# A recurrent cell fused with a gated layer: the first two slots of four chunks in another order, and the last store in halves

## The chip, the cores and the metric

The kernel runs on one core of one Trainium2 chip. A core has a matrix engine (PE, with its weight loads shown as PEld), a vector engine (DVE), an activation engine (ACT), a general engine (POOL), and a queue engine (SP) that issues most transfers; ACT and POOL issue some too. Each engine works through its own list of instructions in order and waits on semaphores for the others. Matrix products land in PSUM, everything else lives in SBUF. The metric is the device time of one execution in microseconds; the median of the runs is compared. The granted clock of PE is 1.00 in every stretch of the profile that is quoted here.

## The reference

An mLSTM cell runs over 4 batches, 8 heads and 768 time steps with head size 40; its output, with heads and batch folded, is the input of a feed-forward layer whose activation is `h * cos(h)`.

```python
for t in range(S):
    m_new = max(f[t] + m, i[t])
    f_stab, i_stab = exp(f[t] + m - m_new), exp(i[t] - m_new)
    C = f_stab * C + i_stab * outer(v[t], k[t])
    n = f_stab * n + i_stab * k[t]
    y[t] = sigmoid(o[t]) * (C @ q[t]) / max(abs(n . q[t]), 1)
x = y as (3072, 320)
h = x @ w_in            # 320 -> 2048
out = (h * cos(h)) @ w_out   # 2048 -> 320
```

## The kernel before

**Chunks and cells.** Time is cut into six chunks of 128 steps (`NC` = 6, `C` = 128). A *cell* n = (chunk, batch) is computed in the parallel form of the recurrence: scores of keys against queries (`scores`, L560), times decays (`weigh`, L566), times values plus the carried state (`values`, L586 to L595), a division by the denominator (`normalize_turned`), and an update of the state: `seam` (L701) makes the increment in PSUM, `fade` (L684, POOL) decays the state `st`, `state` (L726, DVE) adds the increment. The last chunk's cells need no new state. `weigh_k` (L481) and `odd_values` (L487) prepare keys and the odd part of the values on POOL; `turn_blocks` (L538) transposes queries and keys on DVE; `scale_q` (L542, POOL) multiplies queries by the carried decay; `decay` (L476) takes exponentials on ACT.

**The layer, one chunk behind.** While the cells of chunk c + 1 are made, the layer runs on chunk c. Its 2048 hidden columns are done in eight *slots* `f2` = 0 to 7 of 256 columns, two to each batch `b`, the first with `i == 0`, the second with `i == 1`. From the third chunk on (`fast` = 2) `both_parts_fast` does this. In each slot, in this order on PE: the up products of a seven-product scheme (`UpFast`, L817 and L833), with two products of the way down as filler between them; in the even slots the cell's `values` and `seam`; then the slot's share of products of the way down (`down_slot`, L1013). In the second slot these are the sixteen *late* products of the chunk before, and the next cell's scores follow them.

**The other engines in a slot.** ACT copies parts of the up products out of PSUM (L825, L826); POOL adds them up (L834 to L836); DVE joins them into the rest (`join`, L842 and L844). Then the nearest whole number of turns is taken (`near`, L757 on ACT), subtracted (`rest`, L760 on DVE), the sine follows (`sin`, L765 on ACT) and the product with h (`gate`: L769 on DVE for one half, L852 on POOL for the other). `sums` (L902 to L905, four adds on POOL or DVE) forms the combinations of two batches that the way down needs. `x_sums` (L801 to L804, POOL) does the like for the next chunk's input, in the eighth slot. `seam_out` (L708) sends a part of the new input from SBUF to SBUF by two transfers on ACT's queue in the odd slots; they stand between the roundings and the sines.

**The order is written by hand.** `tc.manual_schedule()` keeps each engine's instructions in the order of the calls. Where a call stands in `both_parts_fast` sets its place in the list of its engine; waits are added where one instruction needs another. PSUM buffers are taken in turn from small pools: cells use two buffers of `ps_a`, so the two score tiles of the next cell take the buffers of the last cell's values and of its state increment, and the up products use two of `ps_u`.

**The end.** For the last chunk `last_products` lists the products by `k` (the slot) in an order of its own, and `combine_last` adds them up on DVE (`add_turns`, L875) and stores four blocks of 128 tokens and 320 columns: three from SP (L881), the last one from ACT (L1008). The accumulators are `X0`, `X1`, `Y0`, `Y1`, the tile `late` of two column halves, and `own`.

Of the kernel before, what the change touches and what calls it, by code (L numbers as in the profile page):

```python
# [29 lines left out]
def kernel(  # L30
# [20 lines left out]
    nc = tc.nc  # L51

    B, H, S, D = q.shape
    C = 128
# [3 lines left out]
    D1 = D + 1  # L58
# [878 lines left out]
    def last_products():  # L937

        c = NC - 1
        acc[c] = [ps_o.tile([128, 3, HALF], FP, name="acc", tag="o") for _ in range(4)]  # L940
        late[c] = ps_a.tile([128, 2, HALF], FP, name="late", tag="a")
        own[c] = ps_a.tile([128, HALF], FP, name="own", tag="a")
        X0, X1, Y0, Y1 = acc[c]
        L, Z = late[c], own[c].unsqueeze(1)
        T2, T3, T4 = T

        def first(k):
            G0, G1 = (gs[c, 2 * k + e].rearrange("q (p e t) -> q p e t", p=2, e=2) for e in range(2))
            S, B = blocks[:, S_of(c, k):S_of(c, k) + 4], [[wv[:, k, e, h] for h in range(2)] for e in range(2)]
            return [(X0, 0, G0[:, 0, 0], B[0][0]), (X0, 1, G1[:, 0, 0], B[1][0]), (X0, 2, S[:, 0], T2[:, k]),  # L950
                    (Y0, 0, G0[:, 0, 1], T3[:, k]), (Y0, 1, G1[:, 0, 1], T4[:, k]), (Y0, 2, S[:, 2], B[0][1]),
                    (Y1, 1, S[:, 3], B[1][1])]

        def second(k):
            G0, G1 = (gs[c, 2 * k + e].rearrange("q (p e t) -> q p e t", p=2, e=2) for e in range(2))
            S, B = blocks[:, S_of(c, k):S_of(c, k) + 4], [[wv[:, k, e, h] for h in range(2)] for e in range(2)]
            D1, D4 = (blocks[:, D_of(c, k) + i] for i in range(2))
            return [[(X1, 0, G0[:, 1, 0], B[0][0]), (X1, 1, G1[:, 1, 0], B[1][0]), (X1, 2, S[:, 1], T2[:, k])],
                    [(Y1, 0, G0[:, 1, 1], T3[:, k])], [(L, 0, D1, B[0][1]), (L, 1, D4, B[1][1])],
                    [(Z, 0, G1[:, 1, 1], T4[:, k])]]  # L960

        def ordered():
            for k in range(LAST - 1):
                yield from first(k)
                for part in second(k):
                    yield from part
            yield from first(LAST - 1)
            yield from first(LAST)
            for part in zip(second(LAST - 1), second(LAST)):
                for some in part:  # L970
                    yield from some

        left = {id(t): NF // 2 * n for t, n in ((X0, 3), (X1, 3), (Y0, 3), (Y1, 2), (L, 2), (Z, 1))}
        begun = set()
        for t, i, lhs, rhs in ordered():
            left[id(t)] -= 1
            yield t[:, i], lhs, rhs, id(t) not in begun, left[id(t)] == 0
            begun.add(id(t))
# [3 lines left out]
    def combine_last():  # L982
        c = NC - 1
        X0, X1, Y0, Y1 = acc[c]
        lo, hi = slice(0, HALF), slice(HALF, DM)

        def spread_first(X):
            o = [out_tile() for _ in range(2)]
            nc.scalar.activation(out=o[1][:, lo], in_=X[:, 0], func=AF.Copy, scale=TWO_PI)
            add_turns(out=o[0].rearrange("q (h n) -> q h n", h=2), in0=X[:, 1:3], in1=o[1][:, lo].unsqueeze(1).to_broadcast([128, 2, HALF]))  # L990
            return o

        o = spread_first(X0)
        add_turns(out=o[1][:, hi], in0=Y0[:, 0], in1=o[0][:, hi])
        add_turns(out=o[1].rearrange("q (h n) -> q h n", h=2), in0=Y0[:, 1:3], in1=o[1][:, hi].unsqueeze(1).to_broadcast([128, 2, HALF]))
        out_to(c, 1, o[1])
        add_turns(out=o[0][:, hi], in0=Y0[:, 2], in1=o[0][:, hi])
        p = spread_first(X1)
        add_turns(out=o[0][:, hi], in0=Y1[:, 1], in1=o[0][:, hi])
        out_to(c, 0, o[0])  # L1000
        o, L = p, late[c]
        add_turns(out=o[1][:, lo], in0=Y1[:, 0], in1=o[0][:, hi])
        add_turns(out=o[1][:, hi], in0=L[:, 0], in1=o[1][:, lo])
        add_turns(out=o[0][:, hi], in0=L[:, 0], in1=o[0][:, hi])
        add_turns(out=o[0][:, hi], in0=L[:, 1], in1=o[0][:, hi])
        out_to(c, 2, o[0])
        add_turns(out=o[1][:, lo], in0=own[c], in1=o[1][:, lo])
        nc.scalar.dma_start(out=out[3 * S + c * C:3 * S + (c + 1) * C], in_=o[1])  # L1008

    def run(made, n):  # L1010
        for _ in range(n):
# [489 lines left out]
    def both_parts_fast(c, b):  # L1501

        n = (c + 1) * B + b
        cell, follows = n < N, n + 1 < N
        first = (c, b) == (fast, 0)
        ahead = {0: 3, B - 1: 2}.get(b, H - 2)
        pool = nc.gpsimd if cell else nc.vector
        for i in range(2):
            f2 = 2 * b + i
            up = UpFast(c, f2, lambda: fill_in(c, f2))  # L1510
            if f2 == 0:
                if cell:
                    place_gates(c + 1)
                if cell and not first:
                    odd_values(n)
                    weigh_k(n)
                sin_next()
            if f2 == 2 * B - 2 and c + 2 < NC:
                sigmoid_in_place(c + 2)
                sin_next()  # L1520
            if cell and i == 0:
                if first:
                    scores(n)
                    scale_q(n)
                else:
                    values(n)
                    seam(n)
                    if f2 > 0 and follows:
                        turn_blocks(n + 1)
                if follows:  # L1530
                    decay_exponents(n + 1)
            if cell and i == 1:
                if follows:
                    decay(n + 1, range(ahead, H))
                    sin_next()
                    if f2 > 1:
                        scores(n + 1)
                if n % 2 == 1 and n + 3 < N:
                    load_two(n + 3)
                if b == B - 1:  # L1540
                    x_sums(c + 1)
                elif follows:
                    weigh_k(n + 1)
                    odd_values(n + 1)
                    scale_q(n + 1)
            up.join()
            for e in range(2):
                up.near(e)
            for e in range(2):
                up.rest(e)  # L1550
            if first and i == 0:
                weigh(n)
            if f2 == 2 and cell:
                combine_late(c - 1)
            if cell and i == 0 and not first:
                fade(n)
            if cell and i == 1:
                seam_out(n)
            for e in range(2):
                up.sin(e)  # L1560
                up.gate(e)
            if f2 == 0 and follows:
                turn_blocks(n + 1)
            if f2 == 0:
                sums(c, 0, pool)
            if f2 == 2:
                sums(c, 1, pool)
            down_slot(c, f2)
            if f2 == 1 and follows:
                scores(n + 1)  # L1570
            if f2 == 0:
                for p in range(2):
                    combine_first(c - 1, p)
                for p in range(2):
                    combine_x(c - 1, p)
            if cell and i == 0:
                if follows:
                    decay(n + 1, range(ahead))
                if first:
                    values(n)  # L1580
                    seam(n)
                    fade(n)
                normalize_turned(n)
                if n + 2 < N:
                    load_blocks(n + 2)
                if n + 3 < N:
                    load_E(n + 3)
                if b == B - 2 and c + 2 < NC:
                    load_o(c + 2)
            if i == 0:  # L1590
                if cell:
                    state(n)
                if f2 > 0:
                    sums(c, f2)
            if i == 1:
                if follows:
                    if b == B - 1:
                        scale_q(n + 1)
                    weigh(n + 1)
                if b == 0:  # L1600
                    combine_y(c - 1)
                    if not cell:
                        combine_late(c - 1)
                else:
                    sums(c, f2)
# [42 lines left out]
```

## Time and profile before

| | us |
|---|---|
| median of 3 runs (lowest, highest) | 505.79 (505.65, 506.99) |
| profiled execution | 507.92 |
| its span | 506.1 |
| PE busy | 495.6 (98%) |
| DVE busy | 423.4 (84%) |
| ACT busy | 332.9 (66%) |
| POOL busy | 299.4 (59%) |

The profiled execution is 1.8 us longer than its span, and 2.1 us longer than the median of the three runs. Times inside the profile are counted from the span's start. Two columns of the timeline matter: the start of a group of equal instructions and the time from its start to its end; where an engine stood idle before a group, brackets say for how long and what it waited for. Line numbers name the line of the kernel that issued an instruction; a helper such as `run` (L1013) issues products for many callers, so the tile names tell which ones they are (`acc`, `late`, `own` for the way down; `pup` for the way up).

### The profile page before, as it was taken

Reading aid. Unit: us, or ns where it says so; the run is one execution under the profiler, and the core shown is the slowest. Engines: PE = TensorE matmul, PEld = TensorE weight load, DVE = VectorE, ACT = ScalarE, POOL = GpSimd, SP = SyncE. Lnnn points to the kernel's source line nnn. Section 1 sums busy time; section 2 is a strip of 40 time slices with the busy share of each in tenths; the row PEclk is TensorE's granted clock in tenths of the full one; section 3 lists DMA queues with packets and bytes.
Section 4 is the critical chain, followed back from the end, with each engine's and each line's share of the span. In section 5 each row is a group of like instructions: output and inputs, shape, how many; then the busy total and the mean of one; then the engine's idle time right before and its main releaser. Section 6 shows DMA issues by size and latency. Waiting matters only on the chain.

```text
span 506.1 us, 11146 instructions
## 1 busy us (share of the span) xinstructions
PE 495.6 (98%) x4038; PEld 374.6 (74%) x4038; DVE 423.4 (84%) x842; ACT 332.9 (66%) x646; POOL 299.4 (59%) x394
## 2 busy tenths in 40 slices
PE   9999999999999999999999999999999999999996
PEld 6856645465667668887887788788688878787876
DVE  7889987999887888899889989889979966777655
ACT  6799988888554576754877756777747643444541
POOL 8354656575645666877657967666857456434340
PEclk9999999999999999999999999999999999999999
DMA  9988899998366436129546119628113000010001
GB/s 140 178 215 235 208 219 249 227 230 167 96 172 118 114 109 136 49 77 196 142 116 115 43 42 209 168 70 161 43 33 85 1 6 5 2 53 0 2 0 54
DMA packets 100519, 56.74 MB, mean 112 GB/s; under 512 B 63440, under 2 KB 93216, under 8 KB 100464
## 3 DMA queue, kind: packets, MB, share of 16 engines
q1 hardware_dynamic: 97408, 54.43, 46.7%
q10 hardware_dynamic: 2752, 1.23, 0.9%
q8 instruction: 32, 0.52, 0.5%
q0 software_dynamic: 304, 0.36, 0.3%
q14 instruction: 23, 0.19, 0.1%
HBM read 50.66 MB, written 4.10 MB: 108 GB/s over the span
## 4 chain that ended last, share of the span: by engine, by line
PE 65%; DMA 10%; DVE 9%; SPq 6%; ACT 5%; issue 3%; POOL 1%; ACTq 0%; DVEq 0%
PE acc L1013 19%; PE pup L817 14%; PE pup L749 7%; PE pup L833 5%; PE late L1013 4%; DMA blocks<-in_moe_w_in_dram 4%; PE ps L560 3%; PE po L863 3%; DMA kr<-in_k_dram 2%; PE pup L743 2%; DMA vs<-in_v_dram 2%; DVE n L760 2%; ACT n L757 2%; PE vt L595 2%; PE vt L586 1%
## 5 line engine op out<-in xcount | busy, mean ns | idle before, releaser
L757 ACT ACTIVATE n<-pup 128x512 int32<-128x512 f32 x64 | 36.9, 594 | 85.9 <-DVE pup L842 61.2
L852 POOL TENSOR_TENSOR g<-g,n 128x512 f32<-128x512 f32 x31 | 39.6, 1276 | 54.0 <-ACT n L765 52.0
L765 ACT ACTIVATE n<-n 128x512 f32<-128x512 f32 x96 | 57.9, 627 | 17.2 <-DVE n L760 11.8
L749 PE MATMUL pup<-xT,w_in_sb 128*128 128x512 f32 x128 | 58.8, 602 | 2.2 <-DVE g L769 2.0
L760 DVE SCALAR_TENSOR_TENSOR n<-pup,n 128x512 f32<-128x512 f32 x64 | 43.1, 689 | 19.8 <-ACT n L757 17.5
L1013 PE MATMUL acc<-w_out_sb,g 128*128 128x160 f32 x320 | 58.5, 302 | 0.0
L1013 PE MATMUL acc<-T,g 128*128 128x160 f32 x304 | 56.4, 301 | 0.0
L834 POOL TENSOR_TENSOR blocks<-blocks 128x256 f32<-128x256 f32 x32 | 25.7, 803 | 50.7 <-ACT blocks L826 50.7
L817 PE MATMUL pup<-xT,w_in_sb 128*128 128x256 f32 x192 | 53.5, 385 | 0.2
L476 ACT ACTIVATE E<-E,tab 128x128 f32<-128x128 f32 x160 | 50.1, 389 | 4.3 <-POOL E L462 4.1
L1013 PEld LDWEIGHTS acc<-w_out_sb,g 128*128 128x128 f32 x320 | 49.0, 190 | 4.5 <-issue 2.7
L749 PEld LDWEIGHTS pup<-xT,w_in_sb 128*128 128x128 f32 x128 | 23.0, 189 | 32.9 <-issue 32.2
L1013 PEld LDWEIGHTS acc<-T,g 128*128 128x128 f32 x304 | 46.5, 190 | 1.1 <-issue 0.4
L769 DVE TENSOR_TENSOR g<-pup,n 128x512 f32<-128x512 f32 x64 | 42.7, 687 | 5.2 <-ACT n L765 4.4
L817 PEld LDWEIGHTS pup<-xT,w_in_sb 128*128 128x128 f32 x192 | 33.6, 189 | 9.7 <-ACT blocks L826 4.5
L825 ACT COPY blocks<-pup 128x512 f32<-128x512 f32 x32 | 18.7, 583 | 32.3 <-PE pup L817 32.2
L817 PE MATMUL pup<-x_room,room 128*128 128x256 f32 x128 | 38.5, 382 | 0.0
L1013 PE MATMUL acc<-T,blocks 128*128 128x160 f32 x160 | 36.2, 308 | 0.2 <-POOL blocks L904 0.2
L863 PE MATMUL po<-w_out_sb,g 128*128 128x320 f32 x128 | 36.2, 436 | 0.1
L833 PE MATMUL pup<-xL,w_in_l 64*128 64x512 f32 x128 | 36.1, 641 | 0.0
L542 POOL TENSOR_TENSOR qG<-t,G 128x512 f32<-128x512 f32 x20 | 25.5, 1277 | 16.7 <-DVE t L538 16.7
L1013 PE MATMUL acc<-w_out_sb,blocks 128*128 128x160 f32 x160 | 33.8, 301 | 0.0
(227 smaller groups left out, 1208.3 us busy)
## 6 DMA issues: line engine op xcount, KB each, us to landing
E<-M_d SPq DMA_DIRECT2D x20, 512.0 KB, 6.2
qr<-in_q_dram SPq DMA_DIRECT2D x72, 80.0 KB, 2.5
kr<-in_k_dram SPq DMA_DIRECT2D x72, 80.0 KB, 2.1
bits<-in_moe_w_out_dram SPq DMA_DIRECT2D x8, 640.0 KB, 6.8
G<-G_d SPq DMA_DIRECT2D x18, 256.0 KB, 6.4
blocks<-in_moe_w_in_dram SPq DMA_DIRECT2D x32, 128.0 KB, 4.6
out_dram<-o_sb SPq DMA_DIRECT2D x23, 160.0 KB, 1.8
o<-in_o_gate_dram SPq DMA_DIRECT2D x40, 80.0 KB, 3.9
```

Source lines behind the costliest of these rows:

```text
L476: nc.scalar.activation(out=Es[n][:, h], in_=Es[n][:, h], func=AF.Exp, scale=-1.0, bias=tab[:, c, 0, g:g + 1])
L749: nc.tensor.matmul(pu.rearrange("p (b t) -> p b t", b=B), w_in_sb[:, i, ts(2 * f2 + e, 128)], xT[c][:, i:NK * B:NK], start=(i == 0 and not ...
L757: nc.scalar.activation(out=self.n[e], in_=self.pu[e], func=AF.Copy, bias=0.25)
L760: nc.vector.scalar_tensor_tensor(out=self.n[e].bitcast(FP), in0=self.pu[e], scalar=0.25, in1=self.n[e], op0=OP.add, op1=OP.subtract)
L765: nc.scalar.activation(out=r, in_=r, func=AF.Sin, scale=TWO_PI_DOWN)
L769: nc.vector.tensor_tensor(out=g, in0=self.pu[e], in1=self.n[e].bitcast(FP), op=OP.mult)
L817: nc.tensor.matmul(bank[:, part].rearrange("p (b t) -> p b t", b=B // 2), w[:, f2], x, start=start, stop=stop, skip_group_check=True)
L833: nc.tensor.matmul(pu, w_in_l[r, f2], xL[c][r].rearrange("p b t -> p (b t)"), start=False, stop=True, skip_group_check=True)
L834: nc.gpsimd.tensor_tensor(out=s[:, 1], in0=s[:, 1], in1=s[:, 0], op=OP.add)
L852: tt(out=self.g, in0=self.g, in1=self.n[e].bitcast(FP), op=OP.mult)
L863: nc.tensor.matmul(po[c][b], gs[c, f][:, ts(b, C)], w_out_sb[:, f], start=(f == 0), stop=(f == NF - 1))
L1013: nc.tensor.matmul(a, lhs, rhs, start=start, stop=stop)
```

## The change

In `both_parts_fast`, that is in chunks three to six:

- `weigh` of the very first cell stands before the rounding of its slot, not behind it.
- `odd_values` of a chunk's first cell is called at the end of the eighth slot before it, where `scale_q` stood; `scale_q` is called right after `x_sums` in that slot. Before, `odd_values` stood behind the up products of the first slot.
- `sums(c, 0)` on POOL, and `fade` of the very first cell, are called in the second slot behind `scale_q`, not at the end of the first slot. In chunk six, which has no cells, `sums(c, 0)` stays where it was, on DVE.
- `state` of each chunk's first cell is called in the second slot, behind the gate, not at the end of the first one. In the later batches it stays.

In `last_products` the four late products of the last two slots come by column half. In `combine_last` the last block's right half is stored as soon as it is added up, and the left half at the end; before, one store took both.

```diff
-                    [(Y1, 0, G0[:, 1, 1], T3[:, k])], [(L, 0, D1, B[0][1]), (L, 1, D4, B[1][1])],
+                    [(Y1, 0, G0[:, 1, 1], T3[:, k])], [(L, 0, D1, B[0][1])], [(L, 1, D4, B[1][1])],
...
         add_turns(out=o[1][:, hi], in0=L[:, 0], in1=o[1][:, lo])
+        nc.scalar.dma_start(out=out[3 * S + c * C:3 * S + (c + 1) * C, hi], in_=o[1][:, hi])
...
-        nc.scalar.dma_start(out=out[3 * S + c * C:3 * S + (c + 1) * C], in_=o[1])
+        nc.scalar.dma_start(out=out[3 * S + c * C:3 * S + (c + 1) * C, lo], in_=o[1][:, lo])
...
                 if cell and not first:
-                    odd_values(n)
                     weigh_k(n)
...
                 if b == B - 1:
                     x_sums(c + 1)
+                    if follows:
+                        scale_q(n + 1)
                 elif follows:
                     weigh_k(n + 1)
                     odd_values(n + 1)
                     scale_q(n + 1)
+                if b == 0:
+                    if first:
+                        fade(n)
+                    sums(c, 0, pool)
             up.join()
+            if first and i == 0:
+                weigh(n)
             for e in range(2):
                 up.near(e)
             for e in range(2):
                 up.rest(e)
-            if first and i == 0:
-                weigh(n)
...
             if f2 == 0 and follows:
                 turn_blocks(n + 1)
-            if f2 == 0:
+            if f2 == 1 and cell:
+                state(n)
+            if f2 == 0 and not cell:
                 sums(c, 0, pool)
...
                 if first:
                     values(n)
                     seam(n)
-                    fade(n)
...
             if i == 0:
-                if cell:
-                    state(n)
                 if f2 > 0:
+                    if cell:
+                        state(n)
                     sums(c, f2)
             if i == 1:
                 if follows:
                     if b == B - 1:
-                        scale_q(n + 1)
+                        odd_values(n + 1)
                     weigh(n + 1)
```

## The prediction

> **What bounds the kernel now.** I read the engine table first, then what the matrix engine (PE) waited for from the third chunk on, then the timeline around each of those waits, and last the tail. Names: a *chunk* is 128 time steps, chunk three to six are c = 2 to 5 and start on PE at 194.3, 273.3, 351.9 and about 429; each has eight *slots* of about 10 us, and the change works in the first two.
>
> ```profile
> PE 495.6 (98%) x4038; PEld 374.6 (74%) x4038; DVE 423.4 (84%) x842; ACT 332.9 (66%) x646; POOL 299.4 (59%) x394
> ...
> PE vt L589 <- POOL vr L487: 0.7, 2, 0.4
> PE pup L817 <- ACT blocks L825: 0.5, 1, 0.5
> PE vt L586 <- DVE E L566: 0.4, 1, 0.4
> PE late L1013 <- DVE o_sb L875: 0.3, 1, 0.3
> ```
>
> PE is busy 98% of the span, so DVE, ACT and POOL cost only where PE stands. The other lines (matrix engine's waits from 194 us on: us in all, times, longest) hold about 2 us; four of the six waits lie in the slots that the change reorders. The timeline shows more loss than "idle", because matmul ends are modelled; I count from start to start. In chunk five:
>
> ```profile
> 357.36 0.40 PE L586 MATMUL vt<-E,vs 128*32 128x128 f32 x8
> 357.57 0.40 PE L595 MATMUL vt<-qG,st 128*32 128x128 f32 x8
> 358.34 0.43 PE L589 MATMUL vt<-E,vr 128*32 128x128 f32 x8 [0.37 <-POOL vr L487]
> ...
> 363.14 0.43 PE L1013 MATMUL acc<-T,g 128*128 128x160 f32 x2
> 363.41 0.43 PE L1013 MATMUL acc<-w_out_sb,blocks 128*128 128x160 f32 x2
> 364.38 0.48 PE L817 MATMUL pup<-x_room,w_in_sb 128*128 128x256 f32 x1 [0.54 <-ACT blocks L825]
> ```
>
> Groups of L586/L595 follow each other at 0.22 us; L589 comes 0.77 after its forerunner, so 0.55 is lost. Products of two passes follow at 0.27; L817 comes after 0.97, so 0.70 is lost. The same two places lose 0.55 (279.77) and 0.27 (285.31 to 285.85) in chunk four; chunk three loses 0.52 at 202.74. Together 2.6 us: the most that the slots can give.
>
> Next, the second slot of chunk four on DVE and ACT, and the scores on PE that end it:
>
> ```profile
> 288.30 0.86 DVE L726 TENSOR_TENSOR st<-st,pu 40x128 f32<-40x128 f32 x4
> 289.23 0.43 DVE L842 TENSOR_TENSOR pup<-pup,blocks 128x256 f32<-128x256 f32 x1
> 292.67 0.69 DVE L769 TENSOR_TENSOR g<-pup,n 128x512 f32<-128x512 f32 x1 [0.21 <-ACT n L765]
> ...
> 289.69 0.60 ACT L757 ACTIVATE n<-pup 128x512 int32<-128x512 f32 x1 [0.43 <-DVE pup L842]
> ...
> 293.00 1.16 PE L560 MATMUL ps<-t,t 40*128 40x128 f32 x16
> ```
>
> Today the state adds (L726) end at 289.16, four us ahead of the scores that reuse their PSUM buffer. The gate L769 ends at 293.36, after the scores begin. The change puts the adds behind that gate.
>
> **The change part by part.**
>
> *Chunk three, weights before the rounding.* The two L566 (1.27) go ahead of the two L760. L844 ends at 200.27 and the scores at 200.02, so the first L566 ends about 200.95, before PE arrives (about 202.2): the 0.52 goes. The price: ACT's two sines end at about 203.6 for 202.75, which eats the 0.82 that L825 of the second slot idles today; it starts at 206.4 for 206.26, ends 207.0, and the product behind it can start at 207.05 for 207.42. PE gains about 0.35 there, no more.
>
> *Odd values and scale_q, chunks four and five.* L487 moves from the first slot to the end of the eighth one before, so the 0.55 goes. L542 (1.28) moves ahead of the gate L852 there. DVE's L760 at 350.97 waits today for POOL's L804 (ends 351.24) and runs 0.55 after it; L542 then starts at about 351.8 and ends at 353.1, and the gate starts 0.34 late (352.73 today), ending at 354.35. PE's second filler product, at 354.15, waits for that: 0.2. What follows on DVE:
>
> ```profile
> 354.05 1.48 DVE L902 TENSOR_TENSOR blocks<-g 128x256 f32<-128x256 f32 x1
> 355.56 0.83 DVE L903 TENSOR_TENSOR g<-g 128x256 f32<-128x256 f32 x1
> ...
> 194.73 0.42 DVE L902 TENSOR_TENSOR blocks<-g 128x256 f32<-128x256 f32 x1
> ```
>
> Each of these takes 0.42 with POOL idle (chunk three), 0.83 beside a POOL add, 1.48 beside L542. Without L542, the four (354.05 to 358.13 today) end at about 357.35, 0.75 earlier although L902 starts 0.3 later; but the second join L844 also needs POOL's L836, which I get to 358.0 for 357.86, so L844 starts at about 358.05 for 358.39. Rounding, sines, exponentials and the copy L825 follow in order, so L825 comes 0.35 earlier (bounds 0.1 and 0.75). PE, freed of the 0.55 less 0.2, arrives before it: it gains 0.35 in both chunks, and still waits.
>
> *Sums, fade and state.* The four sums of POOL (L902 to L905, 2.9 us) go from the end of slot one to slot two, behind L542; in chunk three the four fades (1.4) too. POOL then starts L834 as soon as L826 has landed (1.8 us sooner in chunk four: 285.8 for 287.65), and DVE reaches the join without 0.86 of adds. So ACT alone sets the rounding: from L825 to L757 it needs 4.03 (285.24 to the end of the table load and the 0.20 behind it, 289.26). From L757 on: 0.62 to the second, 1.20 to the sine (ACT issues two L708 transfers, 1.12), 0.66 to the gate, 0.69, then four adds 0.87: 4.04. The last add ends 8.07 after L825; unheld, the second pair of scores comes 7.75 after it (7.15 from product to scores, 0.6 before). New wait: PE stands about 0.35 to 0.4, with the rest of the scores and all of slot three queued behind, on DVE L566 and on POOL the next adds.
> Chunk three: L825 at 206.4, adds done 214.5 to 214.85 (there today's sine comes 1.41 behind the second L757, the late end), against today's 214.56 for that pair: 0.15 lost. Bounds: 0.35 gained (no hold), 0.8 lost (gate ends as today, 214.50, plus 0.87).
> Chunk four: L825 at 284.89, adds done 292.96, pair at 293.0 for 293.13: 0.1 gained. Bounds: 0.6 gained, 1.1 lost (gate at 293.36, plus 0.87).
> Chunk five has no state adds (L726 is not issued for the last cells): it keeps its 0.35. Bounds 0 and 1.25.
> The POOL gate of slot two moves behind the sums: about 216.3 for 214.37 in chunk three, unmoved in four and five. Its products run after 225, so this costs nothing; the cover is over 7 us. The moved sums are first read at 222.5 and end by 217: nothing. No DMA moves with any of these steps, and SP's queue is passed by none.
>
> *Tail.* In the built program the first read of the late tile waits for the fourth late product in both versions, so the order by column moves nothing: 0 (if it did, up to 0.34, the idle before 501.73). The halved store does:
>
> ```profile
> 502.56 0.31 DVE L875 SCALAR_TENSOR_TENSOR o_sb<-own,o_sb 128x160 f32<-128x160 f32 x1
> 502.90 0.38 ACTq L1008 DMA_DIRECT2D out_dram<-o_sb  x1
> ...
> 503.00:503.50 0.50, 0.00 (x0) 0.00 (x0) 0.00 (x0) 0.00 (x0) 0.00 (x0) 1.00 0.00 0
> 503.50:504.00 0.50, 0.00 (x0) 0.00 (x0) 0.00 (x0) 0.00 (x0) 0.00 (x0) 1.00 0.95 338
> 504.00:504.50 0.50, 0.00 (x0) 0.00 (x0) 0.00 (x0) 0.00 (x0) 0.00 (x0) 1.00 0.85 315
> ```
>
> The last two stores (160 KB from SP, 160 KB from ACT) fill the DMA engines at some 330 GB/s until 504.5. The new store of 80 KB is issued at 502.05 (0.38 on ACT's queue, done before 502.90) and runs before 503.5, where they are empty. 82 KB less at 330 GB/s is 0.25. Bounds: 0 (its landing is a fixed delay) and 0.45 (with 0.2 less queueing).
> A rule speaks against it. The Trainium skill (DMA: Bandwidth & Descriptors, "Rules for kernel authors") advises to coalesce small transfers, since a DMA is mostly a fixed cost; its "Anatomy of one DMA" gives about 2.0 us plus the bytes at 436 GB/s, an estimate of 0.19 gained for half the bytes, because the extra fixed cost lies beside the adds. By it the sum would be 0.06 smaller. Our row (160 KB from ACT in 2.0 us from issue to landing) agrees that the fixed part dominates.
>
> *Sum:* +0.15 − 0.1 − 0.35 − 0.25 = −0.55. The profiled execution took 507.92 for its span of 506.1; the span should be about 505.55. The median of the three runs shown is 505.79, 2.1 below that execution, and I take the change off the median: 505.25.
>
> **The rivals.** *The state adds come in time (faster).* If L844 starts 0.6 or more earlier and the sine follows sooner, scores are not held: −0.3, −0.6, −0.7 and −0.3, together −1.9: 503.9. For it: the four DVE sums shorten by 0.75. Against it: L825 to the last add is 8.07, L825 to scores 7.75, both shifting together.
> *The gate of slot two comes no earlier (slower).* Then the adds end 0.87 after 214.50 and 293.36, and hold PE by 0.8 and 1.1: +1.9, less 0.6 if chunk five and the tail gain: 507.1 to 507.7. It decides where the gate gains under 0.65 us. For it: rounding one operand (L760 at 212.41) already takes 1.04 for 0.69 beside POOL, and POOL is now busy from L834 on. Against it: ACT idles 0.43 before L757 waiting only for the join, and the sine is set by ACT.
> *Nothing arrives:* L542 before the gate costs what L487 gives, and the last store has a fixed delay: 505.8.
>
> **How the numbers follow.** Forecast 0.49 (its own range 504.6 to 506.0), adds in time 0.27, gate no earlier 0.19, nothing 0.05. A change under 0.3% (1.5 us) can't be told from none here; forecast and nothing are within it (0.54), the faster rival beyond it (0.27), the slower one mostly (0.19). The range 503.8 to 507.1 leaves out the far halves of both.
>
> **What the new profile would show.** Right: no wait of L589 on L487 in chunks four and five; a first L566 before the first L760 in chunk three; scores (L560) in slot two of chunks three and four with a wait of 0.3 to 0.5 for DVE's L726, none in chunk five; L825 wait in chunk five still there, at 0.1 to 0.4; the eighth slot's gate on POOL 0.3 later than its sine; last store 0.2 to 0.3 sooner after the last add; DVE still starting on the late tile after its fourth product. Wrong: no wait for L726, or one near 1 us; or L825 no longer awaited, which would say that the POOL order was worth more than I took it for.

## The result and the profile after

The changed kernel takes 503.79 us in the median of 6 runs (503.31 to 505.99), the kernel before 506.46 in 6 runs (505.65 to 507.37). The ratio is 0.9954 with a 95% interval of 0.9933 to 0.9975, so it is faster by 0.46%, some 1.3 to 3.4 us. The 0.46% is beyond the 0.3% within which the likeliest case lay; the lower end of the interval (0.25%) is not. The 503.79 stands at the very edge of the range (503.8 to 507.1). That range was set from a median of 505.79 over three runs, so it allowed a gain of 2.0 us; the medians of six runs differ by 2.7.

The profiled execution took 503.72 us for a span of 501.9; the one of before 507.92 for 506.1. Most of that difference of 4.2 is not the change. Chunk three begins on PE at 192.04 after and at 194.34 before, and everything ahead of it is the same code: over the eleven profiles of the experiments below, one execution each, it began anywhere from 191.6 to 196.2. So I compare from there on, from PE's first up product (L817) in each chunk to the next one's, as the timelines of the two traces give their starts:

| from, to | before, us | after, us | moved | predicted |
|---|---|---|---|---|
| chunk three to four | 79.01 | 78.86 | -0.15 | +0.15 |
| chunk four to five | 78.57 | 77.97 | -0.59 | -0.1 |
| chunk five to six | 76.63 | 75.82 | -0.81 | -0.35 |
| chunk six to the last product | 73.39 | 73.38 | -0.01 | 0 |
| last product to the end of the span | 4.12 | 3.87 | -0.25 | -0.25 |
| sum | | | -1.82 | -0.55 |

By slots: chunk three -0.59 in the first and +0.44 in the second, chunk four -0.42 and -0.18, chunk five -0.43 and -0.37, all other slots within 0.05. The change gained 1.8 us where it works, three times what I forecast. The medians differ by 2.7; whether the rest is chance in the first 194 us can't be told, and 1.8 lies in the interval of 1.3 to 3.4.

The engine table of the profile after, and the answer to what PE waited for from 190 us on (us in all, times, longest):

```profile
PE 495.1 (99%) x4038; PEld 375.4 (75%) x4038; DVE 420.6 (84%) x842; ACT 332.5 (66%) x646; POOL 300.0 (60%) x394
...
PE late L1014 <- DVE o_sb L875: 0.3, 1, 0.3
PE pup L817 <- ACT blocks L825: 0.2, 1, 0.2
PE acc L1014 <- POOL blocks L904: 0.2, 1, 0.2
```

The rows are the waits that are left; those of `late` and `acc` are the same in the profile before. The waits for L487 and for the first L566 are gone, and the one for L825 fell from 0.5 to 0.2. The two places of chunk five, on PE after the change:

```profile
354.67 0.40 PE L595 MATMUL vt<-qG,st 128*32 128x128 f32 x8
354.89 0.40 PE L589 MATMUL vt<-E,vr 128*32 128x128 f32 x8
...
359.93 0.43 PE L1014 MATMUL acc<-w_out_sb,blocks 128*128 128x160 f32 x2
360.54 0.70 PE L817 MATMUL pup<-x_room,w_in_sb 128*128 128x256 f32 x2 [0.17 <-ACT blocks L825]
```

L589 follows at 0.22 us, where it took 0.77; L817 follows at 0.61, where it took 0.97 and 0.27 would be free of waiting. One thing is new: PE is held at the scores of the second slot in chunks three and four. No wait row says so, because the scores are one merged group; its length does. Chunk three, then four, timeline after, on DVE and PE:

```profile
210.40 0.69 DVE L769 TENSOR_TENSOR g<-pup,n 128x512 f32<-128x512 f32 x1 [0.62 <-ACT n L765]
211.01 0.86 DVE L726 TENSOR_TENSOR st<-st,pu 40x128 f32<-40x128 f32 x4
...
211.54 1.60 PE L560 MATMUL ps<-t,t 40*128 40x128 f32 x16
...
289.06 0.85 DVE L726 TENSOR_TENSOR st<-st,pu 40x128 f32<-40x128 f32 x4
...
289.83 1.29 PE L560 MATMUL ps<-t,t 40*128 40x128 f32 x16
```

Unheld, this group takes 1.16 (293.00 in the profile before). So the adds, which end at 211.87 and 289.91, hold it by 0.44 and by 0.13.

And the sums of the first slot of chunk four on DVE and POOL, after the change, the place that the prediction sized wrongly:

```profile
271.87 1.28 POOL L852 TENSOR_TENSOR g<-g,n 128x512 f32<-128x512 f32 x1
273.08 0.32 POOL L487 COPY vr<-vs 128x128 f32<-128x128 f32 x1
273.19 0.48 DVE L902 TENSOR_TENSOR blocks<-g 128x256 f32<-128x256 f32 x1
273.70 0.42 DVE L903 TENSOR_TENSOR g<-g 128x256 f32<-128x256 f32 x1
273.82 0.90 POOL L834 TENSOR_TENSOR blocks<-blocks 128x256 f32<-128x256 f32 x1 [0.42 <-ACT blocks L826]
274.04 0.95 DVE L904 TENSOR_TENSOR blocks<-blocks,g 128x256 f32<-128x256 f32 x1
275.03 0.84 DVE L905 TENSOR_TENSOR blocks<-g,blocks 128x256 f32<-128x256 f32 x1
275.66 0.80 POOL L836 TENSOR_TENSOR blocks<-blocks 128x256 f32<-128x256 f32 x1
276.23 0.43 DVE L842 TENSOR_TENSOR pup<-pup,blocks 128x256 f32<-128x256 f32 x1 [0.36 <-PE pup L833]
```

L902 takes 0.48 for 1.48, and L903 0.42 for 0.84. The four need 2.7 us for 4.1. The first join L842 now waits for PE, no longer for them, and POOL's L836 has ended (276.46) when the second join L844 starts at 276.57.

### The profile page after: what moved, and what is told of

It reads as the page before. It is cut to its first block, busy times and chain, and to the rows that moved or that the text cites. A ratio compares the mean times of both kernels' runs of the same rounds, so it can differ in the third digit from the quotient of the medians.

```text
span 501.9 us, 11143 instructions
## 1 busy us (share of the span) xinstructions
PE 495.1 (99%) x4038; PEld 375.4 (75%) x4038; DVE 420.6 (84%) x842; ACT 332.5 (66%) x646; POOL 300.0 (60%) x394
## 4 chain that ended last, share of the span: by engine, by line
PE 85%; ACT 4%; DVE 3%; DMA 2%; SPq 2%; POOL 2%; issue 1%; DVEq 0%; ACTq 0%; POOLq 0%
PE acc L1014 24%; PE pup L817 17%; PE pup L749 9%; PE po L863 6%; PE pup L833 6%; PE late L1014 5%; PE ps L560 4%; PE pup L743 3%; PE vt L595 2%; PE vt L586 2%; PE pu L701 2%; PE ph L576 1%; DMA E<-M_d 1%; DMA vs<-in_v_dram 1%; DVE n L760 1%
## 5 line engine op out<-in xcount | busy, mean ns | idle before, releaser
L757 ACT ACTIVATE n<-pup 128x512 int32<-128x512 f32 x64 | 37.0, 593 | 84.2 <-DVE pup L842 58.4
L760 DVE SCALAR_TENSOR_TENSOR n<-pup,n 128x512 f32<-128x512 f32 x64 | 43.1, 689 | 18.5 <-ACT n L757 15.9
L834 POOL TENSOR_TENSOR blocks<-blocks 128x256 f32<-128x256 f32 x32 | 25.1, 785 | 54.5 <-ACT blocks L826 54.5
L817 PE MATMUL pup<-xT,w_in_sb 128*128 128x256 f32 x192 | 53.5, 385 | 0.2
L825 ACT COPY blocks<-pup 128x512 f32<-128x512 f32 x32 | 18.6, 582 | 34.2 <-PE pup L817 33.8
L817 PEld LDWEIGHTS pup<-xT,w_in_sb 128*128 128x128 f32 x192 | 33.8, 189 | 9.6 <-ACT blocks L826 4.4
L817 PE MATMUL pup<-x_room,room 128*128 128x256 f32 x128 | 38.5, 382 | 0.0
L542 POOL TENSOR_TENSOR qG<-t,G 128x512 f32<-128x512 f32 x20 | 26.4, 1321 | 16.7 <-DVE t L538 16.7
L566 DVE TENSOR_TENSOR E<-ps,E 128x512 f32<-128x512 f32 x46 | 29.5, 682 | 5.8 <-PE ps L560 5.6
```

What stands on the lines that cost most here:

```text
L566: nc.vector.tensor_tensor(out=w, in0=pss[n][j], in1=w, op=OP.mult)
L757: nc.scalar.activation(out=self.n[e], in_=self.pu[e], func=AF.Copy, bias=0.25)
L760: nc.vector.scalar_tensor_tensor(out=self.n[e].bitcast(FP), in0=self.pu[e], scalar=0.25, in1=self.n[e], op0=OP.add, op1=OP.subtract)
L817: nc.tensor.matmul(bank[:, part].rearrange("p (b t) -> p b t", b=B // 2), w[:, f2], x, start=start, stop=stop, skip_group_check=True)
```

## The experiments

My theory after the comparison: each part pays or costs at its own place, and the parts add up. L542 beside DVE's sums is what made PE wait in chunks four and five; the state adds behind the gate are a pure cost. Rivals: the gain needs the parts together, above all POOL's sums out of the first slot; or a part that I held for a cost is where the gain is. Each kernel is compared with the profile of before by the same marks ("between the marks" means from PE's first up product of chunk three to the end of the span). A mark moves by at most about 0.05 between profiles in a slot that no edit touches. Where no time is given below, the kernel was executed only once, and only its marks are used.

**Values and scale_q alone.** The kernel before, with these lines:

```diff
                 if cell and not first:
-                    odd_values(n)
                     weigh_k(n)
...
                     x_sums(c + 1)
+                    if follows:
+                        scale_q(n + 1)
...
                     if b == B - 1:
-                        scale_q(n + 1)
+                        odd_values(n + 1)
```

> The kernel before with the two moves of odd_values and scale_q alone. Marks are PE's first up product of each chunk and slot, against the profile of before. Theory (each part pays in its own place): the wait for L487 goes and the four DVE sums of the first slot shorten, so slot one of chunks four and five is 0.4 shorter each, slot two 0.2 to 0.4 shorter each, chunk three and the tail unchanged: -1.3 to -1.5 us. Rival (POOL's four sums must leave slot one too, else POOL still delays the joins): slot one -0.4 each, slot two 0: -0.8 us or less. A third reading (the parts hide each other): 0.

Measured: -1.57 between the marks, a little beyond the -1.3 to -1.5 expected; chunk four -0.43 and -0.30 in slots one and two, chunk five -0.42 and -0.38, nothing else. In time 504.28 for 505.54, ratio 0.9979 (0.9962 to 0.9995). These two moves alone give most of the net gain of 1.82. POOL's sums need not leave slot one for that, and in chunk four the two moves give more (-0.73) than the whole change (-0.59).

**Sums, fade and state alone.**

```diff
+                if b == 0:
+                    if first:
+                        fade(n)
+                    sums(c, 0, pool)
             up.join()
...
-            if f2 == 0:
+            if f2 == 1 and cell:
+                state(n)
+            if f2 == 0 and not cell:
                 sums(c, 0, pool)
...
-                    fade(n)
...
             if i == 0:
-                if cell:
-                    state(n)
                 if f2 > 0:
+                    if cell:
+                        state(n)
                     sums(c, f2)
```

> The kernel before with sums, fade and state of the first slot moved to the second one alone. Theory: no wait of PE in slot one goes, and the state adds behind the gate hold the scores, so slot two of chunks three and four is 0 to 0.4 longer each and chunk five within 0.1: 0 to +0.8 us. Rival (the moved sums free POOL for the joins, and that is where the gain comes from): slot two of chunks four and five 0.2 to 0.4 shorter each: -0.4 to -0.8 us.

Measured: +0.48 between the marks: slot two of chunk three +0.36, of chunk four +0.12, chunk five -0.04. In time 506.14 for 505.54, ratio 1.0011 (0.9992 to 1.0029), which alone tells nothing. It is a cost, and the size of the holds seen after the change.

**Weigh ahead alone.**

```diff
             up.join()
+            if first and i == 0:
+                weigh(n)
...
-            if first and i == 0:
-                weigh(n)
```

> The kernel before with weigh ahead of the rounding in the very first slot alone. Theory: slot one of chunk three 0.5 to 0.6 shorter, slot two unchanged or 0.1 longer (the state adds are still in slot one, scores are not held): -0.5 us. Rival (ACT's later sines give it back through the copies L825 and L826): -0.1 to 0.1 us over both slots. Nothing in chunks four to six by either.

Measured: -0.60; slot one of chunk three -0.59, slot two and all else unchanged. ACT's later sines give nothing back.

**The halved store alone**, with the late products in the order of before.

```diff
         add_turns(out=o[1][:, hi], in0=L[:, 0], in1=o[1][:, lo])
+        nc.scalar.dma_start(out=out[3 * S + c * C:3 * S + (c + 1) * C, hi], in_=o[1][:, hi])
...
-        nc.scalar.dma_start(out=out[3 * S + c * C:3 * S + (c + 1) * C], in_=o[1])
+        nc.scalar.dma_start(out=out[3 * S + c * C:3 * S + (c + 1) * C, lo], in_=o[1][:, lo])
```

> The kernel before with the last block stored in two halves, the late products in the order of before. Theory: only the time from the last product to the end of the span shrinks, by 0.2 to 0.3, since the order by column changes no wait. Rival (the order by column gives the gain by letting DVE start earlier): 0.

Measured: the stretch from the last product to the end of the span is 3.87 for 4.12, as in the changed kernel. The end of this kernel on ACT's queue and DVE:

```profile
502.03 0.92 DVE L875 SCALAR_TENSOR_TENSOR o_sb<-late,o_sb 128x160 f32<-128x160 f32 x3 [0.34 <-PE late L1014]
502.38 0.37 ACTq L1004 DMA_DIRECT2D out_dram<-o_sb  x1
502.86 0.32 DVE L875 SCALAR_TENSOR_TENSOR o_sb<-own,o_sb 128x160 f32<-128x160 f32 x1
503.21 0.34 ACTq L1009 DMA_DIRECT2D out_dram<-o_sb  x1
```

The first half is issued 0.83 us ahead of the second. DVE's idle 0.34 for the late tile is the same here, in the kernel before, and in the changed kernel with its order by column (497.86, 0.34): that order changes nothing.

**Three parts without sums and state**, and the changed kernel again on the same chip. The first is the changed kernel with this edit, which takes the two moves back:

```diff
-                if b == 0:
-                    if first:
-                        fade(n)
-                    sums(c, 0, pool)
...
-            if f2 == 1 and cell:
-                state(n)
-            if f2 == 0 and not cell:
+            if f2 == 0:
                 sums(c, 0, pool)
```

Fade and state stand in slot one again (these lines are left out here), and the late products are in the order of before.

> The changed kernel without the moves of sums, fade and state: values and scale_q moved, weigh ahead, last store in halves, late products in the order of before. Theory (parts add up by place, and the state adds behind the gate cost): against the profile of before -1.57 - 0.58 - 0.25 = -2.4 us between the marks, 0.6 better than the changed kernel; chunk three -0.6 in slot one and nothing lost in slot two. Rival (the moves of sums and state are needed once the other waits are gone, because POOL then delays the joins): no better than the changed kernel, -1.8 or less.

> The changed kernel unaltered, beside the one without the moves of sums and state, on the same chip. Theory: -1.8 us between the marks as in its first profile, and 0.4 to 0.8 us slower in the median than the kernel of three parts. Rival (its first profile was a lucky one): -0.5 to -1.2 us between the marks. The time before chunk three varies from run to run by about 2 us for every kernel, being the same code.

Measured: three parts -2.32 between the marks, the changed kernel again -1.76 (its first profile: -1.82). Chunk three is -0.59 in slot one and unchanged in slot two; chunk four gains 0.71, chunk five 0.79, the tail 0.27. So leaving the two moves out is better by 0.56. In time the two can't be told apart: 503.80 and 504.23 us, ratios 0.9951 (0.9929 to 0.9973) and 0.9947 (0.9926 to 0.9968) to the kernel before (506.57 beside them); medians and ratios even rank them differently. The 0.56 is smaller than what the first 194 us vary.

**State alone, and sums alone.**

```diff
             if i == 0:
-                if cell:
-                    state(n)
                 if f2 > 0:
+                    if cell:
+                        state(n)
...
+            if f2 == 1 and cell:
+                state(n)
```

Sums alone is the kernel before with only `sums(c, 0, pool)` moved as in the diff of sums, fade and state above.

> The kernel before with the state adds of the first slot moved behind the second slot's gate alone; POOL's sums and fade stay in slot one. Theory (what holds the scores is the gate's end plus 0.87; the sums' leaving slot one makes the gate earlier): the gate ends as before or 0.3 to 0.9 sooner, because the join no longer has the adds in front of it, so the hold is larger than the 0.36 and 0.12 seen with the sums moved: 0.4 to 0.8 in chunk three, 0.3 to 1.1 in chunk four, chunk five unchanged: +0.7 to +1.9 us. Rival (the moved sums on POOL, not the adds, hold the scores): 0.

> The kernel before with POOL's four sums of slot one moved to slot two alone; fade and state stay. Theory: PE is held by none of it and freed of none: 0 within 0.1 us in every chunk. Rival (the sums on POOL in slot one delay the joins and through them PE): slot two of chunks four and five 0.2 to 0.4 shorter each. Second rival (the sums in slot two, not the adds, hold the scores in the kernel that moves all): slot two of chunks three and four longer by 0.3 and 0.1.

Measured, state alone: +2.10, more than the +1.9 that I had allowed; slot two of chunk three +0.93, of chunk four +1.14, the rest unchanged. The end of slot two of chunk three in this kernel, on DVE and PE, with a wait row this time:

```profile
215.71 0.69 DVE L769 TENSOR_TENSOR g<-pup,n 128x512 f32<-128x512 f32 x1 [0.36 <-ACT n L765]
216.31 0.84 DVE L726 TENSOR_TENSOR st<-st,pu 40x128 f32<-40x128 f32 x4
...
216.34 0.48 PE L560 MATMUL ps<-t,t 40*128 40x128 f32 x2
217.31 1.12 PE L560 MATMUL ps<-t,t 40*128 40x128 f32 x14 [0.48 <-DVE st L726]
```

The gate ends 20.16 us after the start of chunk three here (216.40 less 196.24), and 20.16 before (214.50 less 194.34): taking the adds away from in front of the join did not bring the gate forward at all, where I had allowed up to 0.9. In this kernel the join waits 0.54 for POOL's add L835 (212.11, `<-POOL blocks L835`), which runs late behind the sums. Sums alone: +0.05, nothing in any slot. So the sums' move does nothing for itself; it pays for most of the state's move (2.10 becomes 0.48) by letting the join, and with it the gate, come earlier: with all three moves the gate ends 0.6 us earlier in chunk three and 1.0 in chunk four, counted from the chunk's start. The move of `fade`, which is made in chunk three alone, was not tried by itself.

**Odd values alone, and scale_q alone.** The first has `odd_values` behind `scale_q` at the end of the eighth slot, and no longer in the first slot; the second only moves `scale_q` to its place right behind `x_sums`. The lines that place `odd_values`:

```diff
                     if b == B - 1:
                         scale_q(n + 1)
+                        odd_values(n + 1)
```

> The kernel before with odd_values moved to the end of the eighth slot, behind scale_q, which stays there. Theory (the copies L825 come late because DVE's sums run beside L542, so PE only waits elsewhere): slot one of chunks four and five 0.4 to 0.55 shorter each, slot two longer by about as much, 0 to -0.3 us in all. Rival (the wait for L487 is a loss of its own): -1.0 us or so.

> The kernel before with scale_q moved ahead of the gate in the eighth slot; odd_values stays in slot one. Theory (L542 beside L902 is the root: without it DVE's four sums, POOL's three adds and L487 behind them all come sooner): slot one of chunks four and five 0.2 to 0.4 shorter each, slot two about 0.3 shorter each: -0.9 to -1.4 us. Rival (the early L542 only delays the eighth slot's gate): 0 to +0.4 us.

Measured: odd values alone +0.01, scale_q alone -1.42, together (above) -1.57. With odd values alone, the wait for L487 only turns into other waits. In chunk four (-0.09 in slot one, +0.12 in slot two) PE waits for the keys of `weigh_k` (L481) instead; in chunk five, which gains 0.57 in slot one and loses 0.55 in slot two, it waits for the copy L825, 1.09 in one piece. PE in chunks four and five, then DVE in chunk five:

```profile
277.74 0.54 PE L701 MATMUL pu<-vs,kw 128*40 128x48 f32 x16 [0.41 <-POOL kw L481]
...
361.66 0.70 PE L817 MATMUL pup<-x_room,w_in_sb 128*128 128x256 f32 x2 [1.09 <-ACT blocks L825]
...
351.35 1.48 DVE L902 TENSOR_TENSOR blocks<-g 128x256 f32<-128x256 f32 x1
352.86 0.42 DVE L903 TENSOR_TENSOR g<-g 128x256 f32<-128x256 f32 x1
...
354.94 0.42 DVE L842 TENSOR_TENSOR pup<-pup,blocks 128x256 f32<-128x256 f32 x1
355.64 0.69 DVE L844 TENSOR_TENSOR g<-pup,blocks 128x512 f32<-128x512 f32 x1 [0.28 <-POOL blocks L836]
```

L902 takes 1.48 as before, since L542 still runs beside it. With scale_q alone (chunk four):

```profile
273.83 0.43 DVE L902 TENSOR_TENSOR blocks<-g 128x256 f32<-128x256 f32 x1
274.29 0.42 DVE L903 TENSOR_TENSOR g<-g 128x256 f32<-128x256 f32 x1
274.63 0.96 DVE L904 TENSOR_TENSOR blocks<-blocks,g 128x256 f32<-128x256 f32 x1
275.62 0.83 DVE L905 TENSOR_TENSOR blocks<-g,blocks 128x256 f32<-128x256 f32 x1
276.87 0.43 DVE L842 TENSOR_TENSOR pup<-pup,blocks 128x256 f32<-128x256 f32 x1 [0.42 <-PE pup L833]
```

L902 takes 0.43, the join waits for PE, and even L487, which stays behind POOL's three adds, now comes early enough that PE does not wait for it.

**State adds ahead of the gate.** The changed kernel with `state(n)` of the second slot between rounding and sine, and the very first `fade` back in slot one:

```diff
+            if f2 == 1 and cell:
+                state(n)
             for e in range(2):
                 up.sin(e)
                 up.gate(e)
...
-            if f2 == 1 and cell:
-                state(n)
```

> The changed kernel with the state adds between the rounding and the gate of slot two, where DVE idles for the sine, and the very first fade back in slot one. Theory (the scores are held by the place of the adds behind the gate): slot two of chunk three 0.4 shorter and of chunk four 0.1 shorter than in the changed kernel: -2.3 us against before, equal to the kernel of three parts. Rival (the later gate holds slot three's first up product, or POOL's work in slot two holds the adds anyway): -1.8 us or worse.

Measured: -2.41 between the marks; slot two of chunks three and four as in the kernel of three parts (0 and -0.31), and the scores take 1.16 again (212.80 and 290.64). DVE has room there, as after the change it idles 0.6 and 0.5 for the sine; the gate ends 0.2 and 0.3 later than after the change and holds nothing. It was the place behind the gate that cost, not the move to slot two.

## Why the prediction was right or wrong

**What bounds the kernel: right.** The 0.55, 0.70 and 0.52 of PE time named in the timeline were the ones that could go. Of 2.6 us in the three chunks the change took 2.1 (0.59, 0.42 + 0.31 and 0.43 + 0.37; the 0.31 is the 0.18 seen plus the hold of 0.13, and agrees with the 0.30 of values and scale_q alone) and gave back 0.6.

**Odd values and scale_q: the mechanism right, a size off; this is the step that failed.** "L825 comes 0.35 earlier (bounds 0.1 and 0.75)". Counted from the chunk's start it came 0.72 earlier in chunk four (11.18 for 11.90) and 0.81 in chunk five (11.05 for 11.86). The term that set the 0.35 was POOL's L836, "which I get to 358.0 for 357.86": it was to end 0.14 later than before and to hold the join L844. It ended 0.37 and 0.39 earlier, counted in the same way, and held nothing; L844 came 0.8 earlier, behind a join that waited for PE. The prediction does not show how the 358.0 is added up, and its rows give less: the gate's end at 354.35, 0.49 for L487 and 2.67 for the three adds (355.19 to 357.86 before) make 357.5, and at that L836 would not have held L844.
Two smaller sizes were off beside it. L542 was to start at 351.8, once DVE's L760 was done, and to end at 353.1; it started right behind L804 and stretched to 1.72, but ended 0.16 sooner than that, counted from the chunk's start, so the gate on POOL was 0.16 late and not 0.34. And L487 took 0.32 and 0.30, not the 0.50 and 0.49 of before.
The four sums on DVE were sized too long as well: 0.75 earlier was forecast for their end, 1.25 came. I let each of the last three take 0.83 beside a POOL add. But POOL's first add L834 waits for ACT's copy L826, which ended at 273.74 in chunk four; L903 had begun by then, and took 0.42. PE's second filler product lost 0.13 for the 0.2 that I allowed.
I also gave the 0.55 of L487 its own line. The run with odd values alone shows that it is none: without the move of scale_q it turns into a wait for L481 or for L825 (+0.01 in all). Each saves only what the next limit lets through.

**Weights before the rounding: right in kind, too cautious.** All of the 0.59 arrived, not 0.35. I had L825 start at 206.4, 12.06 after the chunk's start; it came at 11.58, since the two products of DVE cost the rounding 1.04 and not 1.27, and the sines ended 0.6 late, not 0.85.

**Sums, fade and state: the new wait is there, and it costs.** The hold was put at 0.35 to 0.4 in both chunks; it is 0.44 and 0.13. From L825 to the last add I counted 8.07; chunk four shows 7.84 (282.07 to 289.91), 3.93 of it to the rounding L757, not 4.03, and 3.91 from there, not 4.04. The gain of chunk four came out larger because L825 was earlier and the hold smaller.
**The slower rival was priced rightly, and did not decide.** "the adds end 0.87 after 214.50 and 293.36, and hold PE by 0.8 and 1.1" is what the kernel with the state move alone does: 0.93 and 1.14, the gate just as late as before. In the changed kernel the sums leave slot one, and the gate ends 1.1 and 1.8 earlier, counted from the chunk's start, where that rival needed less than 0.65.
**The faster rival** had the total nearly right (-1.9), and three of its four parts: -0.59 for -0.6 in chunk four, -0.81 for -0.7 in chunk five, -0.25 for -0.3 in the tail; chunk three gave -0.15 for -0.3. But its reason, scores that are not held, did not come about: L844 of the first slot started 0.8 earlier in chunks four and five, as it asks, and the scores were held all the same. The gain came from L825. That the total lies so near to this rival is luck.

**The tail: right.** 0.25 by the halved store, and 0 by the order by column: DVE idles 0.34 for the late tile in either order. The Trainium skill (DMA: Bandwidth & Descriptors, "Anatomy of one DMA") gives a fixed cost of about 2.0 us plus the bytes at 436 GB/s, fitted to transfers that GpSimd issues. For this store, which ACT issues, it made an estimate of 0.19; the 0.25 measured decides, and the profile page has 1.7 us from issue to landing for the 80 KB half and 2.0 for the 160 KB of before. The Trainium skill's advice to coalesce many small transfers into a large one ("Rules for kernel authors" in the same page) does not carry over to this store: split, the span ends sooner, with the first half issued 0.83 us ahead of the second. Whether the fewer bytes at the end or less queueing behind SP's store give the 0.25 was not tried apart.

**The sum** was -0.55 for -1.82. The size of one chain, L542 to L825, accounts for some 0.7 of the 1.27 missing (0.24 in chunk four, 0.46 in chunk five), the smaller hold of chunk four for 0.2, chunk three for 0.3. The median fell by more than the marks, and I had no term for the first 194 us.

## What to carry to other kernels

A wait of the bounding engine is worth only what the next limit leaves: look for the instruction that makes the *next* wait late, and move that one. Here one POOL instruction taken out from beside four vector adds gave 1.4 us by itself, where the whole change gave 1.8; the wait for L487 went with it, and the one for L825 fell from 0.5 to 0.2. Work put behind a gate that itself stands behind other engines belongs ahead of it, in the stretch where its engine idles. And where early work varies by more than the change, compare marks inside the profile, from the first instruction that the change can touch.

## What the runs showed of the hardware

DVE adds of 128x256 with both inputs in SBUF took 0.42 alone, 0.83 to 0.95 beside POOL adds, and 1.48 beside L542 of 1.28; POOL's adds of the same size took 0.73 alone and 0.79 to 0.93 beside them. In the 1.48, L902 began 0.08 behind L542 and ended 0.28 behind it (chunk five before). Where DVE began first, POOL was the longer one: in its new place, late in the eighth slot, L542 took 1.73 and 1.72. The first of these, after the change:

```profile
269.96 0.82 DVE L760 SCALAR_TENSOR_TENSOR n<-g,n 128x512 f32<-128x512 f32 x1
270.19 1.73 POOL L542 TENSOR_TENSOR qG<-t,G 128x512 f32<-128x512 f32 x1
```

The Trainium skill (SBUF — State Buffer, "Who interferes with whom") says that a vector instruction with two SBUF inputs contends with a POOL instruction that reads SBUF, that the port pair they share is an exclusive lock, and that the order of issue decides which of the two blocks. The traces agree, with the 1.48 of L902 begun second and the 1.73 of L542 begun second.

The time of the first two chunks, the same code in every kernel here, varied by 4.6 us between profiles (191.6 to 196.2 at the start of chunk three), while a slot of the later chunks repeated within 0.05. The three latest starts (194.6, 195.3 and 196.2) belong to the three profiles that moved the least by DMA in their first 50 us, 182 to 187 GB/s for 192 to 199 in the others; in two of these three, but not in the third, PE's granted clock was 0.97 there. What makes the first part vary was not tried.
